# The largest weight over all partitions: a transposition, a maximum and a product in place of two trips through DRAM, and longer planned durations for the gate

## The chip, the cores and the metric

The kernel runs on one core of a Trainium2 chip. Its time is the device time of one launch in microseconds (us). TensorE (PE) multiplies matrices, VectorE (DVE) and ScalarE (ACT) work element by element, GpSimd (POOL) takes some of that work, and SyncE (SP) starts the transfers. Every engine executes its own list of instructions strictly in the order written, and waits at an instruction whose inputs aren't there.

## The reference

Attention with a decay over 8 batches, 8 heads, 576 tokens and 64 elements a head, and then a feed-forward network (FFN) with a softplus gate over all 4608 tokens:

```python
scores = scale * np.matmul(q, k.transpose(0, 1, 3, 2))
log_f = np.log(np.clip(f, 0.0001, 1.0))
cum = np.cumsum(log_f, axis=-1)
decay = cum[:, :, :, None] - cum[:, :, None, :]
scores = np.where(causal, -1000000000.0, scores + decay)
...
attn = attn / (np.sum(attn, axis=-1, keepdims=True) + 1e-09)
x = np.matmul(attn, v)   # then heads side by side: 4608 x 512
h = x @ w_in                                        # 512 x 2048
g = np.maximum(h, 0.0) + np.log1p(np.exp(-np.abs(h)))
out = g @ w_out                                     # 2048 x 512
```

## The kernel before, in words

The work is a list of some thousand small operations. Attention comes as a list of jobs (two jobs of four heads, four of two, and from then on one head each), the FFN as 11 blocks of 128, 256 or 512 tokens. Nothing is written out in the order in which the engines do it: `Plan` holds for every operation the engines that could do it (`On`, with a cost in us and a bias), what it follows, and which buffers it takes. `Plan.run` goes through planned time, picks the operation that can start first, gives it to the engine with the lowest planned end, and emits it. So the costs in the table of helpers (`on_act`, `on_dve`, `scales`, `subs`) set both the engine and the place in each engine's list, and a step that in truth takes longer than planned makes its engine wait in that place, with all that is behind it. Where PE's planned list has a gap over 0.5 us before the first FFN output, `fill_gap` puts products there that nobody uses.

At the beginning the weights arrive as 64-bit numbers: 16 tiles of `w_in` (`sti`) and 16 of `w_out` (`sto`), 512 KB each. POOL, ACT and DVE turn each into 32-bit numbers in five instructions (`load_f64`: scale, clip, low, sign, join). The two FFN blocks of the first 256 tokens use these directly ("plain" blocks, products in 32 bit). For all others each weight is scaled by a power of two and split into a high and a low half of 16 bit (`split_w_in`, `split_w_out`), and for that the largest weight is needed: of each of the four groups of four `w_in` tiles, and of all 16 `w_out` tiles. `largest` reduces a tile to one number a partition (L558 on ACT, L560 on DVE, into `sizes_w`), and `find_top`, five times, finds the largest number of all partitions: L578 reduces `sizes_w` to one column `tops`; L581 stores the column, 128 times 4 bytes, to a scratch in DRAM (`top_d`); L586 loads it back to every partition as a row of 128; L589, on DVE, takes the maximum of that row; L593 to L597, on DVE, make the scales (`w_tops`, `w_up`, `w_down`) of it. Both transfers stand in SP's one list, between the loads of q, k, v and weights.

A neighbouring step gets a largest number in another way: `spread_sizes` (L808 to L823), for v, transposes 8 columns on PE, reduces on DVE, and spreads the results to all partitions by a product on PE.

The gate of the FFN (`gate`) is a chain for each tile of 128 x 512: Exp (L1570) and Ln (L1573) on ACT, a scaling (`scales`, L256 on ACT or L258 on DVE or POOL), a combination with h on DVE (L1580), the high half (`scales` again), and the low half on DVE (`subs`, L1594). L1539 are the FFN's first products (h), L1617 its second (acc); for plain blocks L1520 and L1636. In attention L1082 and L1087/L1088 are scores, L1262/L1265 turns of the weights, L1318 and L1397 products with v.

Of the kernel before, what the change touches and what calls it, by code (L numbers as in the profile page):

```python
# [241 lines left out]
def scales(n):  # L242

    return [
        On("DVE", 0.11 + n / 1920, SCALE_BIAS), on_act(n, 0.09), On("POOL", 0.24 + n * 0.0026),
    ]


def subs(n):

    return on_dve(n, port=True)
# [14 lines left out]
def tile_decay_attention_softplus_ffn(  # L266
# [145 lines left out]
    top_d = dpool.tile([(NG + 1) * P], F32, name="top_d")  # L412
    sizes_w = cpool.tile([P, 2, NFC], F32, name="sizes_w")
    tops = cpool.tile([P, NG + 1], F32, name="tops")
    junk = cpool.tile([P, NCH * D], F32, name="junk")
    cpool.tile([P, 32], F32, name="gap")
# [8 lines left out]
    )  # L425
    top_ops, top_set, out_set = {g: [] for g in range(NG + 1)}, {}, []
# [124 lines left out]
    def largest(i, k, x, on):  # L551
        at = sizes_w[:, k, i : i + 1]

        def size(e):
            if hasattr(e, "activation"):
                if "w" not in unused:
                    unused["w"] = buf("vpk", [P, 2, NCH * D], "unused").rearrange("p a b -> p (a b)")[:, 0:DM]
                e.activation(unused["w"], x[i], AF.Abs, accum_out=at)  # L558
            else:
                e.tensor_reduce(at, x[i], AX.X, ALU.max, apply_absolute_value=True)  # L560

        o = add(on, size, after=[(w_out_ready if k else w_in_ready)[i]])
        (w_out_read if k else w_in_read).setdefault(i, []).append(o)
        g = NG if k else i // NCC
        top_ops[g].append(o)
        if len(top_ops[g]) == (NFC if k else NCC):
            find_top(g)
        if sum(map(len, top_ops.values())) == 2 * NFC:
            give("vpk", top_ops[NG])

    def find_top(g):
# [8 lines left out]
        def store(e):  # L580
            e.dma_start(out=top_d[g * P : (g + 1) * P].rearrange("(p k) -> p k", p=P), in_=tops[:, one])  # L581

        def spread(e):
            box["all"] = buf("fe", [P, 512], f"tops{g}")[:, 0:P]
            x = top_d[g * P : (g + 1) * P]
            e.dma_start(out=box["all"], in_=bass.AP(x.tensor, x.offset, [[0, P], [1, P]]))  # L586

        def top(e):
            e.tensor_reduce(w_tops[:, one], box["all"], AX.X, ALU.max)  # L589

        def scales_(e):
            x, u, d = w_tops[:, one], w_up[:, one], w_down[:, one]
            e.tensor_scalar(x, x, 2.0 ** (-97 if g == NG else -48), 2.0**100, ALU.max, ALU.min)  # L593
# [6 lines left out]
        o = add_dma(store, 1, after=[o])  # L600
        o = add_dma(spread, 64, after=[o], takes=("fe",))
        o = add(On("DVE", 0.21), top, after=[o])
        give("fe", [o])
        top_set[g] = add(On("DVE", 0.4), scales_, after=[o])
        if g == NG:
            out_set.append(top_set[g])
# [851 lines left out]
    def ffn_block(i):  # L1458
# [102 lines left out]
        def gate(u):  # L1561
# [35 lines left out]
            a = add(on_act(512, 0.0 if plain else 0.09, psum=True), exp, after=need, takes=("fe",))  # L1597
            a = add(on_act(512), log, after=[a])
            if not plain:
                a = add(scales(512), grow, after=[a])  # L1600
            a = add(on_dve(512), total, after=[a], takes=("gh",) if plain else ())
# [24 lines left out]
        def down_part(u, k, tiles=range(ntile)):  # L1626
# [23 lines left out]
            if plain:  # L1650
                w_out_read.setdefault(fc, []).append(op)
                if i == NPB - 1:
                    splits_left.append(lambda: split_w_in(fc))
                    out_splits.append(lambda: split_w_out(fc))
# [68 lines left out]
    plain_units = []  # L1723
# [94 lines left out]
    for n in range(len(jobs) + 1):  # L1818
        cur, nxt = att[n], att[n + 1]
# [31 lines left out]
        if n >= S_FROM:  # L1851
            for _ in range(S_EACH // 2):
                if splits_left:
                    splits_left.pop(0)()
# [9 lines left out]
        if n >= nstart:  # L1864
            for x in (splits_left, out_splits):
                while x:
                    x.pop(0)()
# [45 lines left out]
```

## Time and profile before

| | before |
|---|---|
| runs | 1147.22 us median of 3 (1145.31 to 1148.05) |
| the profiled execution | 1147.06 us, of these 1144.9 us span from the first to the last instruction |
| PE busy | 1063.4 us, 93% |
| DVE busy | 863.0 us, 75% |
| ACT busy | 860.7 us, 75% |
| POOL busy | 295.3 us, 26% |
| granted TensorE clock, mean | 0.969 of 2.4 GHz |

How to read it: the profile and the runs are of the same kernel, and the 2.2 us between the span and the execution's time lie outside of what the trace shows. A busy share over the whole span hides that the stages differ: up to about 175 us weights arrive and the first jobs run, then attention and FFN are interleaved up to about 960 us, and at the end FFN alone is left. A granted clock of 1.00 is 2.4 GHz, 0.50 is 1.2 GHz; values between are means over a stretch.

### The profile page before, as it was taken

Reading aid. Unit: us, or ns where it says so; the run is one execution under the profiler, and the core shown is the slowest. Engines: PE = TensorE matmul, PEld = TensorE weight load, DVE = VectorE, ACT = ScalarE, POOL = GpSimd, SP = SyncE. Lnnn points to the kernel's source line nnn. Section 1 sums busy time; section 2 is a strip of 40 time slices with the busy share of each in tenths; the row PEclk is TensorE's granted clock in tenths of the full one; section 3 lists DMA queues with packets and bytes.
Section 4 is the critical chain, followed back from the end, with each engine's and each line's share of the span. In section 5 each row is a group of like instructions: output and inputs, shape, how many; then the busy total and the mean of one; then the engine's idle time right before and its main releaser. Section 6 shows DMA issues by size and latency. Waiting matters only on the chain.

```text
span 1144.9 us, 17816 instructions
## 1 busy us (share of the span) xinstructions
PE 1063.4 (93%) x5708; PEld 592.1 (52%) x5708; DVE 863.0 (75%) x2209; ACT 860.7 (75%) x1988; POOL 295.3 (26%) x390
## 2 busy tenths in 40 slices
PE   8768969998999899998999899989998999999998
PEld 6556746774555455544555455545544554444443
DVE  7576859889988898898789888898989976322232
ACT  5666858997987788888788887787778876655554
POOL 3122213232324243333223333344323211000000
PEclk9879989998999899999999899999999999999999
DMA  7858853344775566567456566576546433000000
GB/s 210 199 127 198 188 81 80 100 128 122 176 175 127 146 179 148 145 146 174 117 134 157 142 146 145 134 174 145 134 120 169 94 81 70 37 1 1 37 1 37
DMA packets 230732, 140.92 MB, mean 123 GB/s; under 512 B 192448, under 2 KB 209760, under 8 KB 230640
## 3 DMA queue, kind: packets, MB, share of 16 engines
q1 hardware_dynamic: 230472, 139.65, 50.4%
q8 instruction: 45, 0.74, 0.3%
q14 instruction: 47, 0.39, 0.1%
q10 hardware_dynamic: 168, 0.15, 0.0%
HBM read 73.60 MB, written 10.62 MB: 74 GB/s over the span
## 4 chain that ended last, share of the span: by engine, by line
PE 45%; DVE 25%; ACT 16%; issue 6%; DMA 6%; POOL 3%; DVEq 0%; POOLq 0%; SPq 0%; ACTq 0%
PE h L1539 16%; PE acc L1617 15%; DVE cross L1187 5%; ACT p L1120 5%; DVE s L1092 4%; DVE e L1580 3%; ACT gh L256 2%; DMA top_d<-tops 2%; ACT e L1570 2%; PE h L1520 2%; PE o L1397 2%; DVE x L1421 2%; ACT e L256 2%; PE s L1087 2%; PE o L1318 2%
## 5 line engine op out<-in xcount | busy, mean ns | idle before, releaser
L1617 PE MATMUL acc<-wo,gh 128*128 128x512 f16 x1632 | 382.0, 381 | 4.3 <-DVE gh L1594 3.4
L1539 PE MATMUL h<-xh,wi 128*128 128x512 f16 (+1 forms) x1152 | 354.8, 373 | 23.0 <-DVE x L1421 7.5
L1539 PEld LDWEIGHTS <-wi 128*128 128x128 f16 x1728 | 162.7, 99 | 201.5 <-issue 46.0
L1617 PEld LDWEIGHTS <-gh 128*128 128x128 f16 x1632 | 151.4, 98 | 180.5 <-DVE gh L1594 6.9
L1120 ACT ACTIVATE p<-s,negm 128x288 f32<-128x288 f32 (+7 forms) x384 | 182.9, 479 | 64.0 <-DVE negm L1092 56.3
L1539 PE MATMUL h<-xl,wi 128*128 128x512 f16 (+1 forms) x576 | 213.3, 374 | 3.5 <-DVE xl L1494 3.2
L1580 DVE SCALAR_TENSOR_TENSOR e<-e,h_large,h 128x512 f32<-128x512 f32 x136 | 100.7, 741 | 114.3 <-ACT e L256 111.6
L1187 DVE SCALAR_TENSOR_TENSOR cross<-p,rsum,cross 128x512 f16<-128x512 f32 (+4 forms) x288 | 152.9, 573 | 9.5 <-ACT cross L256 5.7
L256 ACT ACTIVATE gh<-e,h_g 128x512 f16<-128x512 f32 x135 | 97.5, 722 | 68.1 <-DVE e L1580 67.0
L1092 DVE CUSTOM_DVE_ANT_0 s<-s,cmask 128x288 f32<-128x288 f32 (+6 forms) x320 | 135.2, 441 | 9.3 <-PE s L1082 2.8
L1570 ACT ACTIVATE e<-h,h_down 128x512 f32<-128x512 f32 x136 | 92.8, 683 | 65.4 <-PE h L1539 61.1
L1594 DVE SCALAR_TENSOR_TENSOR gh<-e,h_g,gh 128x512 f16<-128x512 f32 x136 | 103.5, 761 | 48.7 <-ACT gh L256 47.9
L1087 PE MATMUL s<-T 128*64 128x64 f32 x336 | 126.0, 386 | 7.6 <-ACT p L1120 4.3
L262 POOL CAST T<-raw 128x576 fp32r<-128x576 f32 x63 | 48.6, 779 | 279.7 <-PE s L1087 254.4
L258 POOL TENSOR_SCALAR cross<-p,rsum 128x64 f16<-128x64 f32 (+4 forms) x120 | 111.2, 941 | 27.7 <-DVE rsum L1140 17.6
L1088 PE MATMUL s<-T 68*64 68x64 f32 x336 | 97.9, 296 | 0.0
L1573 ACT ACTIVATE e<-e 128x512 f32<-128x512 f32 x144 | 90.5, 628 | 2.6
L256 ACT ACTIVATE cross<-p,rsum 128x512 f16<-128x512 f32 (+3 forms) x160 | 83.8, 573 | 6.3 <-DVE rsum L1140 5.8
L256 ACT ACTIVATE e<-e,h_up 128x512 f32<-128x512 f32 x113 | 81.4, 721 | 2.3
L1397 PE MATMUL o<-cross,v 128*128 128x64 f16 (+4 forms) x528 | 79.7, 285 | 0.9 <-ACT p L1120 0.5
L1087 PEld LDWEIGHTS s<-T 128*64 128x64 f32 x336 | 61.1, 182 | 30.6 <-ACT p L1120 8.9
L1120 ACT ACTIVATION_READ_ACCUMULATOR p<-s,negm 128x1 f32 (+1 forms) x384 | 75.0, 195 | 0.0
(152 smaller groups left out, 1356.0 us busy)
## 6 DMA issues: line engine op xcount, KB each, us to landing
raw<-in_qkT SPq DMA_DIRECT2D x112, 288.0 KB
vr<-in_vR SPq DMA_DIRECT2D x64, 160.0 KB
out<-ob SPq DMA_DIRECT2D x35, 256.0 KB
sti<-in_w_in SPq DMA_DIRECT2D x16, 512.0 KB
sto<-in_w_out SPq DMA_DIRECT2D x16, 512.0 KB
T<-T SPq DMA_DIRECT2D x56, 144.0 KB
vp<-in_vR SPq DMA_DIRECT2D x24, 320.0 KB
T<-in_qkT SPq DMA_DIRECT2D x8, 288.0 KB
```

Source lines behind the costliest of these rows:

```text
L256: e.activation(out, in_, AF.Copy, scale=by)
L258: e.tensor_scalar(out, in_, by, None, ALU.mult)
L1087: e.matmul(o, qA[:, q0:end], kA[:, a:z], start=True, stop=False)
L1092: e.tensor_tensor_reduce(out=box["o"], in0=box["o"], in1=cmask[0:n_q, right - w : right], scale=-0.125, scalar=m0 if i else 3.0e38, op0=AL ...
L1120: e.activation(o, box["o"], AF.Exp, bias=m1, scale=-1.0, accum_out=acc)
L1187: e.scalar_tensor_tensor(to2, of, f_, to1, ALU.mult, ALU.subtract)
L1397: e.matmul(box["ps"][:, w - x.shape[-1] : w], st["v16"][:, c], x, start=i == 0, stop=i == len(todo) - 1,)
L1539: e.matmul(o, l, r, start=m == 0, stop=m == 11)
L1570: e.activation(box["e"], st["h", u], AF.Exp, scale=h_down[:, i, g])
L1580: e.scalar_tensor_tensor(o, box["e"], large, st["h", u], ALU.min, ALU.max)
L1594: e.scalar_tensor_tensor(box["l"], box["e"], up, box["h"], ALU.mult, ALU.subtract)
L1617: e.matmul(st["acc", tt], l, r[fc], start=first and m == 0, stop=last and m == 2,)
```

## The change

`find_top` no longer stores and loads. PE transposes the column `tops` into a PSUM bank (L582 in the new file), DVE takes the maximum of that row into one number (L585), PE multiplies it with ones to spread it to 128 partitions in the same bank (L589), and DVE makes the scales from there (L594 to L598). The operations of `find_top` are also added later to the plan: at the start of the next job, and not as soon as the last tile of a group has been added; the splits of `w_in` wait until the scale of their group is in the plan. In the gate and in `scales` and `subs` planned costs are raised: Exp by 0.10 us, Ln by 0.10, `scales` on ACT by 0.03, the combination from 0.60 to 0.68, `subs` by 0.07.

```diff
 def scales(n):
     return [
-        On("DVE", 0.11 + n / 1920, SCALE_BIAS), on_act(n, 0.09), On("POOL", 0.24 + n * 0.0026),
+        On("DVE", 0.11 + n / 1920, SCALE_BIAS), on_act(n, 0.12), On("POOL", 0.24 + n * 0.0026),
     ]
 def subs(n):
-    return on_dve(n, port=True)
+    return On("DVE", 0.14 + n / 960, 0.0, True)
...
-            find_top(g)
+            tops_left.append((number_of["n"], g))
...
-        def store(e):
-            e.dma_start(out=top_d[g * P : (g + 1) * P].rearrange("(p k) -> p k", p=P), in_=tops[:, one])
+        def turn(e):
+            o = keep_bank(box, "ps", "att", f"top{g}")
+            e.transpose(o[0:1, 0:P], tops[:, one], ident)
+
+        def top(e):
+            e.tensor_reduce(top_row[:, one], box["ps"][0:1, 0:P], AX.X, ALU.max)
 
         def spread(e):
-            box["all"] = buf("fe", [P, 512], f"tops{g}")[:, 0:P]
-            x = top_d[g * P : (g + 1) * P]
-            e.dma_start(out=box["all"], in_=bass.AP(x.tensor, x.offset, [[0, P], [1, P]]))
-
-        def top(e):
-            e.tensor_reduce(w_tops[:, one], box["all"], AX.X, ALU.max)
+            x = top_row[:, one].to_broadcast([1, P])
+            e.matmul(box["ps"][:, 256:257], x, ident[0:1, 0:1], start=True, stop=True)
...
         o = add(On("DVE", 0.1), over, after=top_ops[g])
-        o = add_dma(store, 1, after=[o])
-        o = add_dma(spread, 64, after=[o], takes=("fe",))
-        o = add(On("DVE", 0.21), top, after=[o])
-        give("fe", [o])
+        o = add(on_turn(1), turn, after=[o], takes=("att",), loose=True)
+        o = add(On("DVE", 0.2), top, after=[o], lag=0.8)
+        o = add(On("PE", 0.1), spread, after=[o])
         top_set[g] = add(On("DVE", 0.4), scales_, after=[o])
+        give("att", [top_set[g]], back(box, "ps"))
...
-            a = add(on_act(512, 0.0 if plain else 0.09, psum=True), exp, after=need, takes=("fe",))
-            a = add(on_act(512), log, after=[a])
+            a = add(on_act(512, 0.0 if plain else 0.19, psum=True), exp, after=need, takes=("fe",))
+            a = add(on_act(512, 0.1), log, after=[a])
             if not plain:
                 a = add(scales(512), grow, after=[a])
-            a = add(on_dve(512), total, after=[a], takes=("gh",) if plain else ())
+            a = add(On("DVE", 0.68), total, after=[a], takes=("gh",) if plain else ())
...
+        while tops_left and tops_left[0][0] < n:
+            find_top(tops_left.pop(0)[1])
+        number_of["n"] = n
...
             for _ in range(S_EACH // 2):
-                if splits_left:
-                    splits_left.pop(0)()
+                if splits_left and splits_left[0][0] // NCC in top_set:
+                    split_w_in(splits_left.pop(0)[0])
```

The plan of every engine comes out in a new order. On DVE, before, the second of the five maxima (`w_tops<-tops`) stands behind the conversions and in front of the next scores; `to` and `wol_dt_float` are `w_out` tiles in conversion, `cross<-b` a copy of turned attention weights:

```order
L687 SCALAR_TENSOR_TENSOR wi_3_741<-woh_dt_float_357,w_up,wi_3_741 128x512
L626 TENSOR_SCALAR to_752<-to_752 128x512
L626 TENSOR_SCALAR to_762<-to_762 128x512
L262 COPY cross<-b_1_756 128x384
L589 TENSOR_REDUCE w_tops<-tops_749 128x1
L626 TENSOR_SCALAR to_769<-to_769 128x512
L593 TENSOR_SCALAR w_tops<-w_tops 128x1
```

In the changed kernel the same place on DVE reads so (`s` are scores, whose row minimum is taken, `top_676` is the PSUM bank):

```order
L578 TENSOR_REDUCE tops<-sizes_w 128x1
L627 TENSOR_SCALAR to_665<-to_665 128x512
L1093 ISA s_2_0_672,negm_78<-s_2_0_672,cmask 128x288
L1093 ISA negm_78 128x1
L585 TENSOR_REDUCE top_row<-top_676 1x1
L262 COPY cross<-b_0_678 128x512
L262 COPY cross<-b_1_687 128x384
L644 SCALAR_TENSOR_TENSOR wol_dt_float_663<-to_665,wol_dt_float_663 128x512
L627 TENSOR_SCALAR to_700<-to_700 128x512
L594 TENSOR_SCALAR w_tops<-top_676 128x1
```

The maximum stands two operations behind `tops`, and the scales five rows behind the maximum, where 13 rows lay between `tops` and the maximum before.

On PE, before, the first jobs' turns (`b`), scores (`s`) and products with v (`o`) follow each other from the 27th row on:

```order
L1082 MATMUL s_0_0_249<-T_72 128x256
L1262 MATMUL b_0_253<-ident,p_640_95 128x128 x2
L1265 MATMUL b_0_253<-ident,cross 128x128
L1262 MATMUL b_1_259<-ident,p_640_95 128x128 x2
L1265 MATMUL b_1_259<-ident,cross 128x128
L1082 MATMUL s_1_256_264<-T_72 128x256
L1082 MATMUL s_0_0_274<-T_72 128x256
```

In the changed kernel two scores are moved ahead of them, and the first transposition of `tops` and its product stand in between:

```order
L1083 MATMUL s_0_0_248<-T_72 128x256
L1083 MATMUL s_1_256_252<-T_72 128x256
L1083 MATMUL s_0_0_256<-T_72 128x256
L1815 MATMUL fill<-cmask 128x128 x36
L582 MATMUL top_355<-ident,tops 1x128
L1815 MATMUL fill<-cmask 128x128 x5
L589 MATMUL top_355<-ident,top_row 128x1
L1263 MATMUL b_0_377<-ident,p_640_95 128x128 x2
L1266 MATMUL b_0_377<-ident,cross 128x128
```

So PE now has the first group's `tops` ahead of the first turn of these jobs, with 36 filling products before it.

## Rows read from the trace of the kernel before

**Rows 1.** Busy time of each engine in the three stretches, core 0: start and end, length, then busy us and (x instructions) of PE, PEld (weight loads), DVE, ACT, POOL, then the granted clock, the DMA engines' busy share and GB/s.

```profile
0.00:175.00 175.00, 138.13 (x865) 103.75 (x866) 121.48 (x355) 114.00 (x291) 38.89 (x72) 0.88 0.71 164
175.00:960.00 785.00, 744.67 (x4005) 406.79 (x4004) 681.07 (x1773) 643.98 (x1549) 256.37 (x319) 0.98 0.57 138
960.00:1145.00 185.00, 180.63 (x841) 81.52 (x838) 60.46 (x83) 102.71 (x150) 0.00 (x0) 1.00 0.07 23
```

**Rows 2.** Waits in the first 175 us: who waited for whom, us in total, times, the longest.

```profile
POOL woh_dt_float L635 <- DMA sti<-in_w_in: 45.6, 14, 12.9
POOL wol_dt_float L635 <- DMA sto<-in_w_out: 38.5, 12, 16.1
DVE w_tops L589 <- DMA tops<-top_d: 33.9, 5, 8.2
...
PE o L1318 <- issue: 10.2, 1, 10.2
...
PE o L1318 <- DVE g L1580: 8.2, 2, 4.2
PE o L1318 <- DVE w_tops L593: 8.1, 1, 8.1
...
PE size L815 <- DVE size_rows L811: 6.4, 1, 6.4
```

**Rows 3.** The chain of work that ended last, in order of time: start, length, what.

```profile
26.41 7.97 DMA top_d<-tops
34.44 5.42 DMA tops<-top_d
...
71.59 10.18 issue
```

**Rows 4.** The instructions in order of time around the second stop: start, length, engine, line, what, and in brackets the idle time before it and what ended it.

```profile
76.67 0.29 DVE L589 TENSOR_REDUCE w_tops<-tops 128x1 f32<-128x128 f32 x1 [7.23 <-DMA tops<-top_d]
...
81.78 2.37 PE L1318 MATMUL o<-cross,vr 128*64 128x192 f32 x18 [10.20 <-issue]
```

**Rows 5.** Stretches of 5 us, columns as in rows 1: one in which the first store of `tops` was under way, and those behind the five stops.

```profile
25.00:30.00 5.00, 4.99 (x45) 4.46 (x46) 4.08 (x16) 3.31 (x13) 0.00 (x0) 1.00 0.82 25
...
40.00:45.00 5.00, 4.31 (x13) 2.88 (x14) 4.97 (x19) 3.15 (x9) 0.77 (x1) 0.50 1.02 263
...
80.00:85.00 5.00, 3.22 (x22) 2.74 (x23) 4.90 (x15) 4.56 (x9) 1.52 (x2) 0.50 0.24 56
85.00:90.00 5.00, 5.00 (x33) 4.84 (x32) 4.21 (x9) 5.00 (x15) 0.77 (x1) 0.75 0.94 302
...
110.00:115.00 5.00, 2.15 (x18) 1.66 (x18) 4.00 (x13) 2.73 (x6) 1.67 (x3) 0.64 0.91 319
115.00:120.00 5.00, 5.00 (x23) 3.40 (x22) 4.90 (x13) 4.23 (x11) 1.44 (x2) 0.68 0.85 265
...
150.00:155.00 5.00, 4.32 (x28) 3.65 (x29) 4.94 (x13) 4.84 (x14) 0.00 (x0) 0.50 0.12 33
...
170.00:175.00 5.00, 2.68 (x6) 1.86 (x7) 4.76 (x21) 3.52 (x9) 2.13 (x2) 0.50 0.01 3
```

**Rows 6.** Instructions in order of time around the conversion of the fourth tile of `w_in` (columns as in rows 4): POOL, ACT and DVE with the tile's steps, or with the same step of a tile next to it, and PE's work in that time, first and last, with two runs of filling products.

```profile
19.03 0.77 POOL L635 TENSOR_SCALAR woh_dt_float<-sti 128x512 uint16<-128x512 uint16 x1 [0.41 <-DMA sti<-in_w_in]
...
19.41 0.68 ACT L623 ACTIVATE ti<-sti 128x512 f32<-128x512 f32 x1
...
20.20 0.42 DVE L626 TENSOR_SCALAR ti<-ti 128x512 f32<-128x512 f32 x1
...
21.60 0.68 DVE L643 SCALAR_TENSOR_TENSOR woh_dt_float<-ti,woh_dt_float 128x512 uint32<-128x512 uint32 x1
...
23.22 0.78 ACT L639 ACTIVATE woh_dt_float<-ti 128x512 f16<-128x512 f32 x1 [1.79 <-DVE ti L626]
...
25.52 0.68 DVE L560 TENSOR_REDUCE sizes_w<-woh_dt_float 128x1 f32<-128x512 f32 x1
...
12.45 0.39 PE L1262 MATMUL b<-ident,p 128*128 128x128 f32 x2
...
17.62 1.28 PE L1814 MATMUL fill<-cmask 128*128 128x128 f32 x10
...
20.19 0.94 PE L1814 MATMUL fill<-cmask 128*128 128x128 f32 x6
...
22.10 0.70 PE L1082 MATMUL s<-T 66*128 66x256 f32 x2
```

**Rows 7.** The neighbouring step of the sizes of v, all over the span: duration in ns, least, median and most, first and last start.

```profile
L815 PE MATMUL size<-ident,size_rows x16: 251/271/374, 172.3 to 815.6; 8*128 8x8 f32 x16
L808 PE MATMUL size<-ident,size x8: 272/273/275, 164.4 to 812.6; 128*8 128x128 f32 x8
```

**Rows 8.** Groups of the gate's instructions, one shape each: count, busy us, mean ns of one, then idle time before them and what ended it.

```profile
L1594 DVE SCALAR_TENSOR_TENSOR gh<-e,h_g,gh 128x512 f16<-128x512 f32 x136 | 103.5, 761 | 48.7 <-ACT gh L256 47.9
...
L256 ACT ACTIVATE gh<-e,h_g 128x512 f16<-128x512 f32 x135 | 97.5, 722 | 68.1 <-DVE e L1580 67.0
L1570 ACT ACTIVATE e<-h,h_down 128x512 f32<-128x512 f32 x136 | 92.8, 683 | 65.4 <-PE h L1539 61.1 <-issue 2.4 <-DVE gh L1594 1.2
L1573 ACT ACTIVATE e<-e 128x512 f32<-128x512 f32 x144 | 90.5, 628 | 2.6
```

More of the change, by code (lines that the diff above doesn't have):

```diff
@@ L411, in tile_decay_attention_softplus_ffn @@
     NG = NFC // NCC
-    top_d = dpool.tile([(NG + 1) * P], F32, name="top_d")
     sizes_w = cpool.tile([P, 2, NFC], F32, name="sizes_w")
     tops = cpool.tile([P, NG + 1], F32, name="tops")
+    top_row = cpool.tile([1, 32], F32, name="top_row")
     junk = cpool.tile([P, NCH * D], F32, name="junk")
-    cpool.tile([P, 32], F32, name="gap")
     w_tops = cpool.tile([P, NG + 1], F32, name="w_tops")
@@ L425, in tile_decay_attention_softplus_ffn @@
     )
+    tops_left = []
     top_ops, top_set, out_set = {g: [] for g in range(NG + 1)}, {}, []
@@ L578, in over @@
             e.tensor_reduce(tops[:, one], x, AX.X, ALU.max)
-        def store(e):
-            e.dma_start(out=top_d[g * P : (g + 1) * P].rearrange("(p k) -> p k", p=P), in_=tops[:, one])
-        def spread(e):
-            box["all"] = buf("fe", [P, 512], f"tops{g}")[:, 0:P]
-            x = top_d[g * P : (g + 1) * P]
-            e.dma_start(out=box["all"], in_=bass.AP(x.tensor, x.offset, [[0, P], [1, P]]))
-        def top(e):
-            e.tensor_reduce(w_tops[:, one], box["all"], AX.X, ALU.max)
+        def turn(e):
[3 more added lines that the diff above has]
+            e.tensor_reduce(top_row[:, one], box["ps"][0:1, 0:P], AX.X, ALU.max)
+        def spread(e):
+            x = top_row[:, one].to_broadcast([1, P])
+            e.matmul(box["ps"][:, 256:257], x, ident[0:1, 0:1], start=True, stop=True)
         def scales_(e):
             x, u, d = w_tops[:, one], w_up[:, one], w_down[:, one]
-            e.tensor_scalar(x, x, 2.0 ** (-97 if g == NG else -48), 2.0**100, ALU.max, ALU.min)
+            top = box["ps"][:, 256:257]
+            e.tensor_scalar(x, top, 2.0 ** (-97 if g == NG else -48), 2.0**100, ALU.max, ALU.min)
             e.tensor_scalar(u.bitcast(U32), x.bitcast(U32), BITS, BITS, ALU.bitwise_and, ALU.bitwise_xor)
@@ L1652, in down_part @@
                 if i == NPB - 1:
-                    splits_left.append(lambda: split_w_in(fc))
+                    splits_left.append((fc,))
                     out_splits.append(lambda: split_w_out(fc))
@@ L1721, in tile_decay_attention_softplus_ffn @@
     ffn, late, splits_left, out_splits = [], [], [], []
-    plain_units = []
+    plain_units, number_of = [], {"n": 0}
     def switch(e):
@@ L1864, in tile_decay_attention_softplus_ffn @@
         if n >= nstart:
-            for x in (splits_left, out_splits):
-                while x:
-                    x.pop(0)()
+            while tops_left:
+                find_top(tops_left.pop(0)[1])
+            while splits_left:
+                split_w_in(splits_left.pop(0)[0])
+            while out_splits:
+                out_splits.pop(0)()
         for at in [a for a in ready_at if a < n]:
```

## The prediction, made before the changed kernel ran

> **What bounds the kernel now.** I read the busy time by stretches first [rows 1]. From 960 us on PE is busy nearly throughout and nothing there is touched by the change. From 175 to 960 us PE is busy for 744.67 of 785 us, so 40.3 us are idle, 5.1%, with DVE at 681.07 (87%) and ACT at 643.98 (82%). Up to 175 us PE is busy for 138.13 us only, idle for 36.9 us, at a mean granted clock of 0.88: the loosest stage per us, and the one in which the five maxima are found. The work of PE is fixed and the later stages are 95% to 98% full of it, so an idle us taken out of the first stage comes out of the end nearly whole, as long as the later stages stay as dense as they are.
>
> Next the waits of that first stage [rows 2]. DVE waits five times, 33.9 us in all, for the row that comes back from DRAM. PE's four largest entries are the echo of it: 10.2, 8.2 in two, 8.1 and 6.4 us, together 32.9 of the 36.9 us of idle time. Of the 10.2 the row says "issue"; the timeline [rows 4] has DVE standing still until 76.67 and PE starting at 81.78, so it is the second of the five stops under another name. The chain of waits [rows 3] shows the price of one trip: 7.97 us for the store of 512 bytes and 5.42 us for the load, 13.4 us. While the store is under way the transfer engines are 0.82 busy at 25 GB/s [rows 5], so it also takes room from the loads. In the same stretch POOL waits for weight tiles 84.1 us in 26 waits [rows 2], the longest of 12.9 and 16.1 us; the load of the row stands in SP's list ahead of weight loads and is held there until the store has landed.
>
> **The change part by part.** The sum is made against the profiled execution, 1144.9 us of span and 2.2 us around it, 1147.1; the median of the runs is 0.2 us higher, which is nothing here.
>
> The five stops go: two transfers each, and with them DVE's wait and PE's. Gain 32.9 us.
>
> Behind each stop PE runs for a while at half its clock: 0.50 at 40 to 45 us, 0.50 and 0.75 at 80 to 90, 0.64 and 0.68 at 110 to 120, 0.50 at 150 to 155 and at 170 to 175 [rows 5]. The time lost is PE's busy time by what is missing of the clock: 2.16 + 1.61 + 1.25 + 0.77 + 1.60 + 2.16 + 1.34 = 10.9 us. Without stops it goes too. Ceiling: 43.8 us.
>
> From that comes off what takes their place.
>
> First, PE waits for `tops` of the first group before it does the work that it did meanwhile. It has only three scores and the filling products before the first transposition (the list in the part on the change). The fourth tile's POOL step starts at 19.03 and its ACT step at 19.41; with 0.68 + 0.42 + 0.78 + 0.68 + 0.68 us for the five steps behind [rows 6], and no DVE work of attention between them, which stood there before (the fourth tile's ACT step waited 1.79 us for DVE), `tops` is there at about 22.7. Until then PE did turns, scores and products from 12.45 to 22.80, less 2.2 us of filling products [rows 6], less two scores that now stand ahead, 0.70 us each: 6.7 us, say 7, of work that now comes later. Price 7 us; at least 0 (where it fits into waits), at most 10.35.
>
> Second, ten new waits: PE waits for DVE before each transposition and each product. The neighbouring step for v has the same four parts [rows 7]. Outside the fifth stop PE lost about nothing at it, since its one large wait of 6.4 us [rows 2] is that stop. But `tops` comes at the end of a chain of loads, which the plan takes to be faster than they are. I take 0.5 us each, 5 us; bounds 0 and, with POOL's mean wait for a tile of 84.1/26 = 3.2 us at each of the five transpositions, 16. What is queued behind such a wait is everything on PE, and DVE's next maximum waits for PE in turn.
>
> Third, density. Between the stops PE was idle for 36.9 - 32.9 = 4.0 us, since the stops let DVE's and ACT's results run ahead of it. Without them DVE has 121 us of work in some 145 us, 84%, close to the 87% of the middle stage. PE's idle share there, 5.1%, on 140 us is 7.1 us: 3.1 us more. Bounds: 0 and, by DVE's work at no more than 87%, 121.5/0.87 = 140 us, which isn't a bound.
>
> Fourth, ten small PE instructions at 0.27 us [rows 7] make 2.7 us. The PSUM bank held from the transposition to the scales is one of the attention's; I take that as nothing, since the ten waits already carry the risk. DVE's maximum and scales cost what they did.
>
> The SP list loses ten entries, two of which each time blocked q, k, v and weight loads behind them; I give no gain of its own for that, it is what lets the stops go without the loads coming in their place.
>
> The planned durations: Exp takes 683 ns, Ln 628, the scaling 722 and the low half 761 [rows 8], against 584, 522, 612 and 604 planned before and 684, 622, 642 and 673 now. The plan then sees ACT fuller: in the new lists ACT has 35 rows fewer (1485 for 1520), DVE 18 more (2227 for 2209), POOL 10 more. ACT had room (82%), DVE less (87%). A plan nearer to the truth should leave fewer waits out of the 40.3 us of the middle; DVE, at about 0.55 us for one of the 18, gets 10 us more to do. I take zero between the two, with bounds of 20 us gained (half of the idle time) and 10 us lost. PE's list has as many FFN products left behind its last attention product as before, but for 24 more of 858; the middle has these fewer, so this cancels.
>
> Sum: 43.8 - 7 - 5 - 3.1 - 2.7 = 26.0. Span 1144.9 - 26 = 1119; with the 2.2 us around it 1121.
>
> [...]
>
> **The rivals.**
>
> Weight loads take the stops' place. The five transpositions wait for tiles as POOL does, 3.2 us each instead of 0.5 + 0.5 with the product: 16 - 5 = 11 us given back, 1132. For it: POOL's 84.1 us. Against: its longest waits lie inside the stops, and the transfer engines' mean share is 0.71 [rows 1], with the stores in it.
>
> DVE is the bound of the middle: 18 more rows on it, 10 us, 1131. For it: 87% busy. Against: ACT gets as much room, and is the other half of every gate.
>
> The plan's better durations pay in the middle: half of 40.3 us, 1101. For it: all four ACT and DVE steps were planned 0.10 to 0.16 us short for 136 tiles. Against: nothing shows that the idle time comes from these.
>
> The stops were cover and the weights' arrival sets the pace of the first stage: no change, 1147. For it: shares of 0.91 and 1.02 in some stretches [rows 5]. Against: 0.71 over the stage. [...]
>
> Slower: PE's list is held at each of the five transpositions as long as DVE's is now at each maximum, 33.9/5 = 6.8 us, because `tops` is as late as its last tile and PE, unlike DVE, has nothing else while it waits. Then 34 us come in the place of 5 and the half clock stays: 26 - 29 - 10.9 = -14, that is 1161. It decides from about 4 us a transposition on, (26 + 5 - 10.9)/5. For it: the transposition stands ahead of all else on PE. Against: in four groups of five it stands behind other work that fills the wait.
>
> **How the numbers follow.** The forecast 0.55, weights 0.14, DVE 0.10, durations 0.10, no change 0.05, slower 0.06. A difference under 0.3% (3.4 us) can't be told from none. Faster: 0.55 + 0.14 + 0.10 + 0.10 = 0.89; same 0.05; slower 0.06. The forecast's own range, from the bounds of its four deductions, is 1108 to 1133. Toward the better durations I take it to 1102, and upward to 1139, past the two rivals that give back 10 to 11 us and with some of both together; left outside are no change, slower, and the far end of the durations, about 0.17.
>
> **What would show it.** Right: no DVE wait over 2 us at the maximum; PE idle for about 15 us before the point that was 175 us, at a clock near 1.00; the first scores of single heads, the first FFN products in 16 bit, and the last attention product each some 25 us earlier; the last stage as long as before. The first transposition should start at about 23 us. Wrong: waits of several us of PE at the new transpositions, POOL still waiting more than 60 us for weights, a middle with more idle PE time than 40 us, or a DVE that is over 90% busy there.

## The result and the profile after

The changed kernel takes 1116.62 us, the median of four runs (1112.65 to 1117.95), against 1147.63 us (1145.31 to 1148.51) of the kernel before on the same chip. The ratio is 0.9727, interval 0.9697 to 0.9757: faster by 2.7%, 31 us. The profiled execution took 1117.95 us, of these 1115.7 us span.

The first view is again the busy time by stretches, for the changed kernel, cut where the first 16-bit product of the FFN starts (149.2 us) and where the tail begins. Columns as in [rows 1].

```profile
0.00:149.20 149.20, 143.20 (x956) 107.10 (x957) 132.47 (x391) 124.16 (x317) 46.76 (x78) 0.99 0.68 199
149.20:931.00 781.80, 737.79 (x3948) 403.49 (x3947) 687.42 (x1757) 622.19 (x1493) 256.29 (x328) 0.97 0.57 138
931.00:1116.00 185.00, 180.30 (x839) 81.47 (x837) 59.03 (x80) 100.25 (x147) 0.00 (x0) 1.00 0.05 18
```

Read the first column against the second: PE's idle time in the first stage is 149.20 - 143.20 = 6.0 us where it was 36.9 [rows 1], the granted clock is 0.99 where it was 0.88, and the transfer engines move 199 GB/s where they moved 164. In the kernel before, the first 16-bit product started at 183.83 us; so this stage ends 34.6 us earlier. The middle did not gain: 44.0 us idle (781.80 - 737.79), 40.3 before. The end of the span comes 29.2 us earlier, so some 5 us went missing behind the first stage.

The waits of the first 149.2 us of the changed kernel, the same view as [rows 2]:

```profile
POOL woh_dt_float L636 <- DMA sti<-in_w_in: 26.6, 15, 9.4
POOL wol_dt_float L636 <- DMA sto<-in_w_out: 13.6, 10, 2.8
...
PE top L582 <- DVE tops L578: 2.7, 1, 2.7
PE warm L1804 <- POOL cmask L451: 2.3, 1, 2.3
PE o L1319 <- ACT cross L262: 1.0, 1, 1.0
```

PE's three waits are all that is left of its idle time here. One of them is new, the 2.7 us before the first transposition. The largest surprise stands at the top: POOL waits 40.2 us for weight tiles where it waited 84.1 [rows 2]. No load was made smaller or moved to another queue; ten entries left SP's list, and the rest of it stands in the order of the new plan.

The timeline of the changed kernel around that first transposition (columns as in [rows 4]):

```profile
13.31 8.20 PE L1815 MATMUL fill<-cmask 128*128 128x128 f32 x72
24.20 0.27 PE L582 MATMUL top<-ident,tops 128*1 128x128 f32 x1 [2.68 <-DVE tops L578]
24.30 1.28 PE L1815 MATMUL fill<-cmask 128*128 128x128 f32 x10
```

And the four steps of all five searches: duration in ns, least, median and most, first and last start, as in [rows 7].

```profile
L589 PE MATMUL top<-ident,top_row x10: 245/255/265, 25.5 to 125.7; 1*128 1x1 f32 x10
...
L582 PE MATMUL top<-ident,tops x5: 269/273/273, 24.2 to 123.0; 128*1 128x128 f32 x5
L585 DVE TENSOR_REDUCE top_row<-top x5: 272/279/280, 24.6 to 124.2; 1x1 f32<-1x128 f32 x5
L594 DVE TENSOR_SCALAR w_tops<-top x5: 134/157/159, 25.9 to 126.9; 128x1 f32<-128x1 f32 x5
```

Transposition, maximum and spreading product are now about 1 us of work (0.273 + 0.279 + 2 x 0.255), where one trip took 13.4 us [rows 3]. The product appears twice for each search (x10), since the trace shows a 32-bit product of this form as two instructions.

### The profile page after: what moved, and what is told of

It reads as the page before. It is cut to its first block, busy times and chain, and to the rows that moved or that the text cites. A ratio compares the mean times of both kernels' runs of the same rounds, so it can differ in the third digit from the quotient of the medians.

```text
span 1115.7 us, 17863 instructions
## 1 busy us (share of the span) xinstructions
PE 1061.3 (95%) x5739; PEld 592.1 (53%) x5739; DVE 878.9 (79%) x2227; ACT 846.6 (76%) x1955; POOL 303.0 (27%) x405
## 4 chain that ended last, share of the span: by engine, by line
PE 44%; DVE 29%; ACT 13%; issue 5%; DMA 4%; POOL 4%; SPq 1%; DVEq 0%; POOLq 0%; ACTq 0%
PE h L1540 17%; PE acc L1618 17%; DVE cross L1188 7%; DVE s L1093 5%; ACT p L1121 4%; DVE e L1581 3%; PE o L1398 3%; DMA sti<-in_w_in 2%; PE s L1088 2%; DVE x L1422 2%; DVE gh L1595 2%; ACT gh L256 2%; POOL cross L258 1%; PE s L1089 1%; PE b L1263 1%
## 5 line engine op out<-in xcount | busy, mean ns | idle before, releaser
L1188 DVE SCALAR_TENSOR_TENSOR cross<-p,rsum,cross 128x512 f16<-128x512 f32 (+4 forms) x288 | 157.1, 583 | 10.1 <-POOL cross L258 6.2
L1088 PE MATMUL s<-T 128*64 128x64 f32 x336 | 130.1, 397 | 13.3 <-ACT p L1121 4.4
L256 ACT ACTIVATE gh<-e,h_g 128x512 f16<-128x512 f32 x127 | 91.4, 720 | 66.9 <-DVE e L1581 66.5
L262 POOL CAST T<-raw 128x576 fp32r<-128x576 f32 x68 | 53.2, 792 | 295.1 <-PE s L1088 277.7
L256 ACT ACTIVATE e<-e,h_up 128x512 f32<-128x512 f32 x128 | 92.0, 719 | 2.4
L1398 PE MATMUL o<-cross,v 128*128 128x64 f16 (+4 forms) x528 | 82.2, 291 | 7.6 <-DVE x L1422 4.3
L1398 PEld LDWEIGHTS <-v 128*128 128x128 f16 x528 | 51.4, 99 | 56.1 <-issue 12.2
L256 ACT ACTIVATE cross<-p,rsum 128x256 f16<-128x256 f32 (+3 forms) x141 | 76.9, 581 | 4.6 <-DVE rsum L1141 3.2
```

The lines of the kernel that those rows point to most:

```text
L256: e.activation(out, in_, AF.Copy, scale=by)
L1088: e.matmul(o, qA[:, q0:end], kA[:, a:z], start=True, stop=False)
L1188: e.scalar_tensor_tensor(to2, of, f_, to1, ALU.mult, ALU.subtract)
L1398: e.matmul(box["ps"][:, w - x.shape[-1] : w], st["v16"][:, c], x, start=i == 0, stop=i == len(todo) - 1,)
```

## The experiments

They ask three things: how the two halves of the change, the new path and the planned durations, share the 2.7%; why a trip through DRAM is so dear, since DVE's wait for it was only the row that one sees first; and whether the deductions of the prediction for the new waits on PE were real. All ratios are to the kernel before, run on the same chip in the same rounds.

### The two halves of the change

**e1_path**: the changed kernel with all five planned durations put back.

```diff
-        On("DVE", 0.11 + n / 1920, SCALE_BIAS), on_act(n, 0.12), On("POOL", 0.24 + n * 0.0026),
+        On("DVE", 0.11 + n / 1920, SCALE_BIAS), on_act(n, 0.09), On("POOL", 0.24 + n * 0.0026),
...
-    return On("DVE", 0.14 + n / 960, 0.0, True)
+    return on_dve(n, port=True)
...
-            a = add(on_act(512, 0.0 if plain else 0.19, psum=True), exp, after=need, takes=("fe",))
-            a = add(on_act(512, 0.1), log, after=[a])
+            a = add(on_act(512, 0.0 if plain else 0.09, psum=True), exp, after=need, takes=("fe",))
+            a = add(on_act(512), log, after=[a])
...
-            a = add(On("DVE", 0.68), total, after=[a], takes=("gh",) if plain else ())
+            a = add(on_dve(512), total, after=[a], takes=("gh",) if plain else ())
```

> The changed kernel with the five planned durations (Exp, Ln, scaling on ACT, combination, low half) put back to those of before; the transposition, maximum and product stay. If the five stops are all of the gain: 1114 to 1120 us, the first 16-bit product of the FFN at 149 to 152 us as in the changed kernel. If the planned durations bring a part of it: 1125 us or more, and the difference lies after the first 16-bit product. If the durations cost time, as DVE got 18 rows more: 1107 to 1113 us.

**e2_costs**: the kernel before with these five durations of the change, and nothing else of it.

> The kernel before with only the five planned durations of the changed one; the trips through DRAM stay. If the stops are all of the gain: 1144 to 1151 us, five waits of DVE for the row from DRAM with 30 us or more in all, the first 16-bit product at about 184 us. If the durations bring a part: 1135 us or less with the stops still there.

Measured: e1_path 1102.5 us, ratio 0.9652 (0.9627 to 0.9676); e2_costs 1159.02 us, ratio 1.0148 (1.0123 to 1.0172). Neither lies where it was expected. e1_path has the sign of its third case, that the durations cost time, but is faster than the 1107 to 1113 us given for it; by its ratio, on the 1147.63 us of the first comparison, it would take 1107.7. e2_costs is slower than both of its cases. So the new path alone gains 3.5%, 40 us, and the durations alone lose 1.5%, 17 us; in the changed kernel they lose 0.9727 - 0.9652 = 0.75%, some 9 us. Each of the five steps is now planned nearer to its traced duration (four of them in [rows 8]; the combination takes 741 ns), and the plan came out worse. e1_path is faster than both kernels.

Where e1_path is better can be read from the stretches, cut at the same two events in both (the first 16-bit product, and the end of the last attention product): first the middle and the tail of the changed kernel, whose first stage is shown above, then the three of e1_path.

```profile
149.20:936.10 786.90, 742.89 (x3976) 406.06 (x3975) 689.96 (x1762) 625.21 (x1497) 256.29 (x328) 0.97 0.56 137
936.10:1115.70 179.60, 175.20 (x812) 78.90 (x808) 56.49 (x75) 97.24 (x142) 0.00 (x0) 1.00 0.05 18
```

```profile
0.00:141.60 141.60, 134.94 (x917) 101.75 (x918) 126.81 (x376) 116.32 (x302) 41.61 (x74) 1.00 0.70 207
141.60:924.50 782.90, 748.70 (x4034) 406.12 (x4034) 694.98 (x1767) 633.67 (x1527) 263.09 (x331) 0.99 0.56 138
924.50:1099.60 175.10, 170.65 (x790) 76.78 (x787) 54.85 (x74) 95.44 (x139) 0.00 (x0) 1.00 0.05 19
```

In the first stage both kernels leave PE idle for 6 to 7 us, and in the tail for 4.4. In the middle e1_path has 34.2 us idle at a clock of 0.99 against 44.0 us at 0.97: the idle time that the durations add lies there. The lengths of the stages themselves can't be compared one by one, since e1_path has 39 PE instructions fewer in the first stage and 58 more in the middle. The old path agrees: the middle of e2_costs has 789.20 - 745.01 = 44.2 us idle, where the kernel before has 40.3.

```profile
188.70:977.90 789.20, 745.01 (x3980) 406.20 (x3980) 694.18 (x1766) 624.20 (x1502) 248.13 (x330) 0.97 0.55 137
```

**e11_gate**, **e15_total**, **e16_explog**: e1_path with some of the durations: all three of the gate (exponential, logarithm, total), the total on DVE alone, the other two alone.

> e1_path with three of the five planned durations (exponential, logarithm and total of the gate); the planned durations of the splits' subtraction and of the scaling on ACT stay as before. If the gate's durations are what costs the 0.75% by which the changed kernel is slower than e1_path: ratio 0.971 to 0.975, about 1109 to 1114 us. If the other two durations cost it: ratio 0.963 to 0.967, as e1_path, about 1101 to 1106 us.

> e1_path with one of the gate's three planned durations, that of the total on DVE (0.68 us). If a DVE that the plan believes to be busier is what makes the 16-bit rows late at the first 16-bit block and gives the 0.7% of e11_gate: ratio 0.970 to 0.974, about 1110 to 1115 us, with the 5 to 6 us wait of PE for xh. If the two durations on ACT do it: ratio 0.963 to 0.967, without that wait.

> e1_path with the other two of the gate's planned durations, exponential and logarithm on ACT. If these cost: 0.970 to 0.974, about 1110 to 1115 us, and e15_total is as e1_path. If the total on DVE costs: 0.963 to 0.967. If each of the two runs is about 0.4% over e1_path, no single duration is to blame, and every other plan than e1_path's comes out some 0.5% slower.

Measured: 1112.03 us, ratio 0.9717 (0.9694 to 0.974); 1111.33 us, 0.97 (0.9672 to 0.9728); 1108.51 us, 0.9683 (0.9665 to 0.9702). The gate's three make up nearly all of the 0.75%, and the two parts of them add up within the noise: 0.48% and 0.31% against 0.65%, though the intervals of both parts still touch that of e1_path. Whether one part carries most of it can't be told from these runs. One stop goes with the gate's three together; here it is in the changed kernel, and below it in e11_gate:

```profile
236.89 0.61 PE L1540 MATMUL h<-xh,wi 128*128 128x512 f16 x1 [5.89 <-DVE xh L258]
```

```profile
238.21 0.61 PE L1540 MATMUL h<-xh,wi 128*128 128x512 f16 x1 [5.37 <-DVE xh L258]
```

It stands in e2_costs too, at 278.63 us and 5.92 us long, and not in e1_path, e15_total or e16_explog, so e15_total and e16_explog lose their 0.5 and 0.3% elsewhere: PE is idle in their middle for 40.4 and 39.5 us, 5 to 6 us more than in e1_path, with no wait longer than 2.2 us. What in the order of the plan makes these is left open.

### Why the trip is dear

**e3_planned**: the kernel before with the two transfers planned as long as the trace shows them, so that DVE's maximum stands far enough back in its list.

```diff
-        o = add_dma(store, 1, after=[o])
-        o = add_dma(spread, 64, after=[o], takes=("fe",))
+        o = add(on_dma(1), store, after=[o], lag=7.4)
+        o = add(on_dma(64), spread, after=[o], takes=("fe",), lag=4.8)
```

> The kernel before, the trips through DRAM as they are, but planned as long as traced: 8.0 us for the store and 5.4 for the load instead of 2.1 and 2.4. DVE's list then has 33 to 36 rows between the column and the maximum where it had 13 to 17. If the cost of a trip is that DVE's list is held in a place that was planned too early: DVE's wait for the row falls under 8 us in all and the time to 1117 to 1127 us. If the trip costs in itself, by late scales, by SP's list held until the store has landed, or by the room that the store takes: 1132 us or more.

Measured: 1152.36 us, ratio 1.0086 (1.0057 to 1.0114). It is even slower than the kernel before. The waits of its first 180 us:

```profile
POOL wol_dt_float L635 <- DMA sto<-in_w_out: 49.0, 13, 20.7
POOL woh_dt_float L635 <- DMA sti<-in_w_in: 38.2, 13, 9.1
...
PE s L1082 <- ACT p L1120: 13.7, 2, 7.3
```

DVE's wait for the row, 33.9 us in [rows 2], is gone from this list, and nothing was won: POOL waits 87.2 us for weights, and PE stands elsewhere. So taking DVE's wait away wins nothing while the transfers stay. The plan also puts the scales later here, so this run alone doesn't say whether it is the transfers that cost; the next runs do.

**e4_stores**: the changed kernel with the five stores put back where they were, read by nobody.

```diff
+        def store(e):
+            e.dma_start(out=top_d[g * P : (g + 1) * P].rearrange("(p k) -> p k", p=P), in_=tops[:, one])
...
         o = add(On("DVE", 0.1), over, after=top_ops[g])
+        add_dma(store, 1, after=[o])
```

> The changed kernel with the five stores of the column to DRAM added again, for which nothing waits and which nothing reads. If the room that a store takes from the loads (engines 0.82 busy at 25 GB/s for about 5 us each) is a part of the old cost: 1122 to 1130 us and POOL's waits for weight tiles well over their 40 us. If only the waits mattered: 1115 to 1120 us, the same within what can be told.

Measured: 1135.12 us, ratio 0.9934 (0.9913 to 0.9955). Five stores of 512 bytes for which no engine waits take back 0.9934 - 0.9727 = 2.1%, 24 of the 31 us. That is more than the dearer of the two theories had given it, and POOL's waits for weights are at 64.6 us in the first 150 us, where the changed kernel has 40.2. Its trace, 2 us at a time, from the issue of the first store at 24.48 us on:

```profile
24.00:26.00 2.00, 1.40 (x12) 1.31 (x12) 1.56 (x5) 0.90 (x3) 0.33 (x1) 1.00 0.15 15
26.00:28.00 2.00, 2.00 (x17) 1.69 (x18) 1.63 (x8) 2.00 (x6) 0.55 (x2) 1.00 1.95 51
28.00:30.00 2.00, 2.00 (x17) 1.16 (x16) 2.00 (x8) 1.94 (x7) 0.00 (x0) 1.00 0.89 53
30.00:32.00 2.00, 2.00 (x14) 1.33 (x12) 1.76 (x8) 1.30 (x5) 0.00 (x0) 1.00 0.83 25
32.00:34.00 2.00, 0.07 (x1) 0.00 (x0) 0.34 (x2) 0.00 (x0) 0.00 (x0) 1.00 0.55 27
```

and the instructions in order of time, the load issued behind the store, and who waits for it:

```profile
24.48 0.34 SPq L582 DMA_DIRECT2D top_d<-tops  x1
24.94 0.35 SPq L625 DMA_DIRECT2D sto<-in_w_out  x1
...
36.92 0.77 POOL L641 TENSOR_SCALAR wol_dt_float<-sto 128x512 uint16<-128x512 uint16 x1 [9.46 <-DMA sto<-in_w_out]
38.09 0.48 PE L1271 MATMUL b<-ident,cross 128*128 128x128 f32 x1 [6.03 <-POOL cross L262]
```

The transfer engines are busy and move next to nothing, 25 to 53 GB/s for eight us. The 512 KB load issued 0.46 us behind the store is there only at 36.9 us; POOL has waited 9.46 us for it, and PE 6.03 us for POOL, which has a copy for the attention behind that tile in its list. This is a stop like that of [rows 4], without anybody waiting for a row.

Two theories remain. Either the small writes keep the transfer engines from the loads behind them, or the loads are late because SP stands before the store until DVE has `tops`. Two runs part them, each with the same place in SP's list. **e9_ready** stores a column of a constant, so that SP doesn't wait but the 128 small writes stay; **e10_one** waits for `tops`, but stores one partition's 4 bytes.

```diff
-            e.dma_start(out=top_d[g * P : (g + 1) * P].rearrange("(p k) -> p k", p=P), in_=tops[:, one])
+            e.dma_start(out=top_d[g * P : (g + 1) * P].rearrange("(p k) -> p k", p=P), in_=ident[:, one])
```

> The changed kernel with five stores again, in the same places of SP's list and in the same form (128 partitions of 4 bytes, 512 bytes in all), but of a column of a constant that has been ready since the start, so that SP does not stand before the store until the largest weights are there. Theory T (the store itself is dear: its 128 small writes keep the transfer engines from the loads behind it): as dear as the stores of e4_stores, ratio 0.990 to 0.997, about 1132 to 1140 us. Theory L (the price is SP's list: SP stands before the store until DVE has `tops`, and the loads behind it are issued late): the stores then cost nearly nothing, ratio 0.971 to 0.977, about 1112 to 1119 us.

```diff
-            e.dma_start(out=top_d[g * P : (g + 1) * P].rearrange("(p k) -> p k", p=P), in_=tops[:, one])
+            e.dma_start(out=top_d[g * P : g * P + 1].rearrange("(p k) -> p k", p=1), in_=tops[0:1, one])
```

> The changed kernel with five stores that wait for the largest weights as those of e4_stores did, but of one partition's 4 bytes instead of 128 partitions'. Theory T (128 small writes on the transfer engines): nearly nothing is paid, ratio 0.971 to 0.977, about 1112 to 1119 us. Theory L (SP's list held until `tops` is there): as dear as e4_stores, ratio 0.990 to 0.997, about 1132 to 1140 us. A value between the two in both this run and e9_ready means that each has a share.

Measured: e9_ready 1121.25 us, ratio 0.9795 (0.9768 to 0.9822); e10_one 1119.48 us, ratio 0.9784 (0.9757 to 0.9811). PE, DVE, ACT and POOL have the same lists in e4_stores and in these two, and SP's differs in the five stores alone, so the comparison is clean: with either half taken away, 1.4 to 1.5% (16 to 17 us) of the 2.1% is gone. Both lie between the two forecasts: neither theory holds alone, and most of the price is paid where both come together. The same stretches in e10_one, whose one-partition store was issued at 24.32 us with the same load behind it:

```profile
24.00:26.00 2.00, 1.56 (x8) 1.59 (x9) 1.43 (x5) 1.08 (x4) 0.19 (x1) 0.59 0.20 31
26.00:28.00 2.00, 2.00 (x11) 1.76 (x11) 0.47 (x5) 0.83 (x2) 0.00 (x0) 0.55 0.95 303
28.00:30.00 2.00, 2.00 (x20) 1.40 (x17) 1.95 (x5) 1.63 (x5) 1.33 (x3) 1.00 0.83 307
```

303 and 307 GB/s in place of 51 and 53. The view of the transfers shows the packets between 24.3 and 34 us, first of e4_stores, then of e10_one:

```profile
DMA packets 226, 0.34 MB, mean 35 GB/s; under 512 B 144, under 2 KB 144, under 8 KB 225
...
q1 hardware_dynamic: 225, 0.33, 89.7%
```

```profile
DMA packets 518, 1.66 MB, mean 171 GB/s; under 512 B 67, under 2 KB 67, under 8 KB 517
...
q1 hardware_dynamic: 517, 1.65, 54.3%
```

The queue's packets take 89.7% of the engines' time in e4_stores for a fifth of the data. Packet by packet the traces show where that time goes. It isn't the small writes themselves: the median packet of 4 bytes takes 9 ns in each of these kernels. It is the packets of the loads behind them: the median one of 4096 bytes takes 159 ns, but behind the first store of e4_stores some take up to 8.7 us. In the first 200 us, packets of more than 2 us number 108 in the kernel before (427 us, summed over the 16 engines), 111 in e4_stores (388 us), 49 in e9_ready (157 us), 1 in e10_one (2.1 us) and none in the changed kernel. So these long packets come with the 128 small writes, and the wait for `tops` alone makes next to none.

In e9_ready, too, the small writes are dear for the transfer engines. The first 150 us of e9_ready, then of e10_one:

```profile
0.00:150.00 150.00, 143.03 (x943) 107.11 (x944) 129.34 (x375) 118.56 (x305) 44.06 (x76) 0.98 0.76 197
```

```profile
0.00:150.00 150.00, 145.07 (x959) 108.57 (x960) 133.00 (x396) 122.45 (x316) 45.14 (x77) 0.99 0.66 198
```

They are busy for 0.76 of the time against 0.66, 15 us more, for the same 197 and 198 GB/s. But e9_ready issues its first store at 18.31 us, behind loads that are still under way, so the loads behind it come 6 us earlier, and at this store they are not held up:

```profile
18.31 0.40 SPq L582 DMA_DIRECT2D top_d<-ident  x1
18.83 0.36 SPq L625 DMA_DIRECT2D sto<-in_w_out  x1
```

```profile
18.00:20.00 2.00, 2.00 (x20) 2.00 (x20) 1.42 (x2) 2.00 (x4) 1.17 (x2) 1.00 1.05 420
20.00:22.00 2.00, 2.00 (x20) 2.00 (x20) 1.97 (x5) 0.92 (x3) 0.78 (x1) 1.00 1.04 305
22.00:24.00 2.00, 0.33 (x3) 0.14 (x2) 1.97 (x4) 1.47 (x3) 0.76 (x1) 1.00 1.09 253
24.00:26.00 2.00, 1.29 (x7) 1.32 (x8) 1.80 (x5) 1.03 (x4) 0.77 (x1) 0.59 1.02 307
```

Its long packets all lie behind the later four stores, and POOL's waits for weights are at 49.8 us in the first 150 us against 64.6 in e4_stores. That tiles which are already there absorb those delays fits this, but no run tests it. In e4_stores the list has first run dry while SP stood before the store (0.15 busy at 24 to 26 us), and then the small writes hold up the first loads that come; e10_one runs dry in the same way (0.20 busy), and its loads then come at 303 and 307 GB/s. Why e9_ready and e10_one are each still 0.6 to 0.7% above the changed kernel is open: the added store puts the plan in another order on every engine, and no run has that order without a store. So of the 2.1% of e4_stores up to 0.7% may be the order, and 1.4 to 1.5% are shown to go when either half of the store's price goes.

The Trainium skill ("DMA: Bandwidth & Descriptors", section on the specifications) gives 512 bytes as the least transfer at line rate, below which the engines read, modify and write. The direction agrees with these runs, eight us at 25 to 53 GB/s behind 128 writes of 4 bytes and 303 to 307 GB/s behind one; the reading and modifying itself no run here shows.

**e17_trip**: e4_stores with the five loads of the row as well, again read by nobody.

```diff
+        def load(e):
+            x = top_d[g * P : (g + 1) * P]
+            e.dma_start(out=buf("fe", [P, 512], f"tops{g}")[:, 0:P], in_=bass.AP(x.tensor, x.offset, [[0, P], [1, P]]))
...
-        add_dma(store, 1, after=[o])
+        d = add_dma(store, 1, after=[o])
+        d = add_dma(load, 64, after=[d], takes=("fe",))
+        give("fe", [d])
```

> e4_stores with the five loads of the row as well (64 KB each, behind the store's end on SP's list as before, read by nobody): the whole trip through DRAM on the list, but without DVE's wait for it. If SP's stand for the store's end (31.5 us in five in the trace of the kernel before) holds up the weights: ratio 1.00 to 1.015, about 1145 to 1160 us, with POOL's waits for weights nearer the 84 us of before. If the store has already cost what there is to cost: within 0.4% of e4_stores, ratio 0.990 to 0.997.

Measured: 1149.81 us, ratio 1.0046 (1.0021 to 1.0071), 1.1% (13 us) above e4_stores. Its waits, SP's own in the first 190 us, and POOL's:

```profile
SPq L586 <- DMA top_d<-tops: 35.3, 5, 8.6
...
POOL woh_dt_float L647 <- DMA sti<-in_w_in: 44.1, 16, 9.9
POOL wol_dt_float L647 <- DMA sto<-in_w_out: 36.5, 13, 14.4
```

SP stands 35.3 us before the five loads until the stores have landed, with the weight loads behind it in its list, and POOL's waits for weights are at 80.6 us, where the kernel before had 84.1 [rows 2]. All of the price of before but its last part is back, with no engine waiting for the row.

So the runs make a ladder, all with the new durations: changed kernel 0.9727; with the stores 0.9934; with the loads too 1.0046; with the row read and awaited on DVE (e2_costs) 1.0148. Of the 4.2% between its ends, 2.1% go to the stores, 1.1% to the loads and SP's stand before them, and only 1.0%, some 12 us, to DVE's wait and the older order. The order of the other instructions changes at each of these rungs, so the parts are good to no more than the 0.6 to 0.7% that e9_ready and e10_one leave open.

### The new waits on PE

**e12_path3** and **e18_now**: e1_path with the first group's search three jobs later in the plan, and e1_path with every search laid into the plan at once, as in the kernel before.

```diff
-            tops_left.append((number_of["n"], g))
+            tops_left.append((number_of["n"] + (3 if g == 0 else 0), g))
```

> e1_path with the search for the first group's largest weight put three jobs later in the plan, so that its transposition stands on PE behind two more blocks' attention products and not behind 36 filling products. If the first group's wait is a cost on the path, as the prediction had it (7 us for the wait, beside the half clock behind it): 0.3 to 0.7% under e1_path, ratio 0.958 to 0.962. If PE stands there for the loads anyway, and filling products cover it: within 0.3% of e1_path, ratio 0.963 to 0.968; and slower than that if the splits that wait for the first group's factors become late.

```diff
-            tops_left.append((number_of["n"], g))
+            find_top(g)
```

> e1_path with the search for the largest weight laid into the plan at once, as before, and not one job later. If the deferral keeps PE from standing before the transposition: slower than e1_path by 0.3 to 1%, ratio 0.968 to 0.975, with waits of several us of PE for `tops` in more than one group. If only the first group waits, as in the changed kernel: within 0.3% of e1_path, ratio 0.963 to 0.968.

Measured: e12_path3 1109.07 us, ratio 0.969 (0.9673 to 0.9706), some 0.4% slower than e1_path, the two intervals just touching; e18_now 1106.31 us, ratio 0.9665 (0.9643 to 0.9687), no difference that can be measured. In e12_path3 PE no longer waits for `tops` at all, and the kernel is not faster: moving the first group's wait out of the way gains nothing. That the wait as such is free doesn't follow, since the plan's order changes with it. In e18_now the same wait has two entries and 6.0 us, where e1_path has one of 2.5:

```profile
PE top L582 <- DVE tops L578: 6.0, 2, 3.2
```

More than double the wait, and no loss that can be measured. The later place of the search in the plan, a part of the change, isn't needed for the gain.

## Why the prediction was right, and where its working was not

The time came out at 1116.6 us for 1121 predicted, inside the range, and on the forecast side of every rival. Part by part:

| step | predicted | what the runs show |
|---|---|---|
| stops and half clock go | 43.8 us | the stage ends 34.6 us earlier; e1_path gains 40 us |
| first group's wait | 7 | 2.7 idle, and 5 us at a clock of 0.66 behind it; in e1_path 2.5 idle at a clock of 1.00, and no gain when it is moved (e12_path3) |
| ten new waits | 5 | none but that one |
| density of the stage | 3.1 | 6.0 us idle in all: nothing |
| small PE instructions | 2.7 | 5 x 0.273 + 10 x 0.255 = 3.9 |
| planned durations | 0 (-20 to +10) | 9 us lost |

That the size is right is luck, for two errors cancel. Three deductions, 15.1 us together, were too large: DVE at 132.47 of 149.2 us is 89% busy, above the 87% of the middle stage from which I had taken the idle share, and PE still waits for next to nothing. And the planned durations, which I set at nothing between two bounds, cost 9 us, near the end of their bounds; the rival that they pay has the wrong sign. My sentence that a plan nearer to the truth should leave fewer waits is the step that failed: on both paths it left more idle time of PE in the middle, 44.0 us against 34.2 on the new one and 44.2 against 40.3 on the old. The range, too, was summed wrongly: the bounds of the four deductions give 1106 (2.7 us alone come off) to 1135 (10.35, 16, 3.1 and 2.7), not 1108 to 1133.

The cause was only half right. I took DVE's 33.9 us for the stop and PE's 32.9 us for its echo, and of SP's list I wrote that "I give no gain of its own for that". e3_planned takes that wait away and loses time; e4_stores and e17_trip give no engine a row to wait for and take back 37 of the 48 us between the ends of the ladder. The row that I cited only in passing, transfer engines 0.82 busy at 25 GB/s while the store is under way [rows 5], was the main one. DVE's wait, PE's echo and POOL's 84.1 us are then for the most part one delay seen on three engines. PE's 32.9 us gave nearly the right size because PE stood still whichever engine held it up: its idle time in the first stage fell by 30.9 us, and POOL's waits for weights fell by 43.9. The clue was there: POOL's longest waits for weights, 12.9 and 16.1 us [rows 2], are longer than any of DVE's waits for the row.

As for the marks: DVE doesn't wait at the maximum at all, and at most 0.7 us at the scales behind it; under 2 us was said. PE is idle for 6.0 us in the first stage, about 15 said. The first transposition at 24.2 us, 23 said. The first 16-bit product 34.6 us and the last attention product (969.8 to 935.9 us) 33.9 us earlier, for 25 said. The last stage was not as long as before, but 4.7 us longer. Behind the last attention product the changed kernel has these products of the FFN, first h, then acc (the first number in brackets counts PE's):

```profile
936.10:1115.70 179.60, 89.10 (x390) 0.00 (x0) 24.65 (x33) 22.67 (x33) 1.00 0.05 18
...
936.10:1115.70 179.60, 96.05 (x420) 0.00 (x0) 3.48 (x5) 5.29 (x8) 1.00 0.05 18
```

These are 810, and the same two rows of the kernel before have 384 and 405, or 789. 21 more at 89.10/390 = 0.228 us are 4.8 us, the 4.7 us by which the tail grew. I had set that off against a middle that has these fewer; but the middle was as long as before (786.9 us between the two events, 786.2 before), since it has 3.7 us more idle PE time and a lower clock (0.97 for 0.98). One of the marks of "wrong" did come true, more than 40 us idle in the middle: 44.0, though the kernel before had 40.3 already. POOL's 40.2 us, far from the 60 us that I had named as a bad sign, settles the rival of the weight loads: without the stores the weights come sooner, not in the stops' place. DVE's busy share of the middle is 88% (687.42 of 781.80), under the 90% that I had named, and e1_path is faster at 89%. And the slower case, PE held for 6.8 us at each transposition, was wrong at each of the five.

## What to carry to other kernels

A wait for a small transfer is not its price: look at what stands behind it in the same list, and at the GB/s while it is under way. A column of 128 partitions stored to DRAM as 4 bytes each cost 3 to 5 us a time here through the loads behind it, although nobody waited for it (16 to 24 us for five); to test such a suspicion, keep the transfer and drop its reader, then drop its small pieces or its wait one at a time. And a table of planned durations need not get better when some of its entries are corrected, as here: change it in a run of its own.

## What was not expected of the hardware

The transfer engines show 0.55 to 1.95 busy while they move 25 to 53 GB/s, for eight us behind a store of 512 bytes in 128 pieces, against 303 to 307 GB/s behind the same store of one piece. Here the busy share says nothing of throughput, since a load's packet of 4096 bytes that takes 8.7 us in place of 0.16 counts as busy for all of it. And one such store is dear or cheap by something that these runs don't settle: e9_ready moves 253 to 420 GB/s from 16 to 26 us, although its first store is issued at 18.31 us; its second, issued at 51.25 us, also with loads ahead of it, is followed by 104 to 129 GB/s at 58 to 62 us.
